# Attention and two expert layers on one core: four edits to the order of work around TensorE's waits

## Chip, cores and metric

The kernel runs on one core of a Trainium2 chip. The metric is the device time of one execution in microseconds (us), taken as the median of several. The engines are TensorE (PE in the profile, its weight loads PEld), VectorE (DVE), ScalarE (ACT), GpSimd (POOL) and SyncE (SP), which issues most transfers.

## What is computed

Three layers follow each other. The reference, cut to what matters:

```python
# 1. attention with a band mask: batch 4, 8 heads, 576 positions, head size 64
scores = (q @ k.T) / sqrt(64)          # heads 0-3: 32 back; heads 4-7: every fourth of 128 back
attn = softmax(where(mask, scores, -1e9))
x = (attn @ v) as [2304 tokens, 512]
# 2. a dense layer with squared ReLU: 512 -> 2048 -> 512
g = s * relu(x @ w_in) ** 2 + b
y = g @ w_out
# 3. eight experts, each token goes to one
logits = normalised(y) @ normalised(expert_emb).T / tau
e = argmax(logits);  gate = softmax(logits)[e]
out[token] = gate * (relu(y @ w1[e]) @ w2[e])
```

## The kernel before, in words

Every large product is made of three passes of TensorE: each operand is split into a rounded high part and a low part that holds the rest, and `mm3` (L459 to L463) adds high by high, and the two cross products. High parts are written by ScalarE, low parts by VectorE, so a product often waits for a low part.

**Groups, steps and slots.** The 2304 tokens are 18 tiles of 128 in five groups: g0 has 4 tiles, g1 has 2, g2 to g4 have 4 each. A group's dense layer has 16 steps, one for each 128 columns of the hidden size. A step has a first product (`gemm1_mm`, into a bank ph of PSUM, then ReLU, square and split) and, two steps later, a second product (`gemm2`), which adds into the group's banks py0 to py3, one for each tile; each py bank exists once. The steps run in the order g0's first half, all of g1, g0's second half, g2, g3, g4. The loop in `main` numbers half steps: slot 2i holds the first product of step i, slot 2i+1 the second product of step i-2. When a group's sixteenth second product is through, four copies (two for g1) take py to SBUF tiles ysb (L518). There are four ysb buffers in all, taken in turn, so a group's copies need the buffers that older groups' tiles leave.

**Attention beside it.** The attention of later groups is cut into pair units n = 8, 10, ... 34 and fitted into these slots by `attn_steps`. Each pair has a load (a), two sets of scores with their maximum and exponentials (b, scores pS by L241, maximum L248 and L251, exponentials L256), a normalisation (norm, L261 to L263), a turn of both probability tiles by transposes into banks pT with their copies (c, L270 and L274), the product with v and the high half of x (d, L284 and L301), and the low half of x (e, L305). `TEMPO` gives a start slot, a period and the offset of c for each group; steps of one slot come in the order a, d, e, c, b, norm. The probability tiles (tag prob) have two buffers; scores, turns and ph take four banks of PSUM in turn.

**Background items.** When a group's y has been copied, `logits_dve` puts a list of items on `self.bg`: for each tile eight dot products with the expert embeddings (VectorE, L761, one instruction of 512 columns each), then a choice of the expert (`choose`, L816 on) and gates. Behind the attention steps of a slot one item is taken from this list (two in odd slots from step 48 on, two in every slot in g4's steps). A group's ysb buffers are free when their last dot has run.

**What sets the order.** TensorE's instructions run in the order in which the program writes them. VectorE's and ScalarE's order in this part is chosen by the scheduler, with one exception: a dot is kept in program order, behind the VectorE instruction that the program wrote just before it. So a dot in a slot whose steps end with norm stands behind that normalisation.

**Experts.** From step 75 on, routing and the first expert's weights are prepared beside the last steps. Then TensorE turns gathered tokens (`xt`, banks px), makes hidden layers (`g1_pair` and `g1`, banks ph) and the second product (`g2`, banks po); `g2` scales po by the gate on VectorE (L1164) and scatters the rows to the output by an indirect transfer that GpSimd issues (L1165). At the very end a count of used slots is read into a register of each engine (`values_load`, L1312) and decides by a branch (L1314) whether more tokens are left; with this data none are.

Of the kernel before, what the change touches and what calls it, by code (L numbers as in the profile page):

```python
# [7 lines left out]
F32 = mybir.dt.float32  # L8
# [3 lines left out]
AF = mybir.ActivationFunctionType  # L12
# [8 lines left out]
NPOS = 2 * NPAIR + NSING + NTAIL  # L21
NUNIT = NPAIR + NSING + NTAIL
# [9 lines left out]
P = 128  # L32
# [77 lines left out]
class Kern:  # L110
# [277 lines left out]
    def attn_steps(self, n0, n1, ps):  # L388


        live = {}
        todo = []
        for n in range(n0, n1, 2):
            g = next(g for g in range(NG) if n // 4 < U0[g + 1])
            start, period, turn = TEMPO[g - 1]
            t = period * ((n - 4 * U0[g]) // 2) + start

            def a(n=n):
                ms = [divmod(n + i, 4) for i in range(2)]
                qks = [self.load_qk(*m) for m in ms]  # L400
                for i, m in enumerate(ms):
                    self.loaded[n + i] = qks[i], self.load_v(*m)
                live[n] = [self.attn_a(*m, ps) for m in ms]

            def each(*fs, n=n):
                def run(n=n):
                    for f in fs:
                        for c in live[n]:
                            f(c)
                return run  # L410

            def d(n=n):
                self.attn_pv(live[n])
                self.attn_hi(live[n])

            def e(n=n):
                self.attn_lo(live.pop(n))

            def b(n=n):
                self.attn_scores2(live[n])  # L420
                each(self.attn_max, self.attn_exp)(n)
            o = t + max(period, turn + 1)
            todo += [(t + LOAD, 0, n, a), (t, 4, n, b),
                     (t + 1, 5, n, each(self.attn_norm)), (t + turn, 3, n, each(self.attn_turn, self.attn_copy)),
                     (o, 1, n, d), (o + (turn < period), 2, n, e)]
        todo.sort(key=lambda x: x[:3])
        return todo
# [110 lines left out]

    def phase1(self, wl, first_pools, late, late_pools):
        tc, nc = self.tc, self.nc  # L540
        self.gt, self.bg, self.ysb, self.raws, self.loaded, self.py = {}, [], {}, {}, {}, {}
        sp_cm = tc.tile_pool(name="sp", bufs=1, side="right")
        self.spool = sp_cm.__enter__()
        ET = mybir.EngineType
        late.enter_context(tc.manual_schedule(engines={ET.PE}))
        with tc.tile_pool(name="psM", bufs=1, space=PSUM, reuse_waits="tile") as self.psM, ExitStack() as man:
            psA_cm = tc.tile_pool(name="psA", bufs=1, space=PSUM, side="right", reuse_waits="tile")
            self.psR = psA_cm.__enter__()
            self.turns, self.psf, self.step = [0, 1, 2, 3], self.bank_a, 0
            man.enter_context(tc.manual_schedule(engines={ET.Activation, ET.DVE}))  # L550
            with tc.tile_pool(name="pp", bufs=1) as self.ppool:
                self.warm = self.ppool.tile([P, 768], BF16, tag="prob", name="warm", bufs=5)[:, :P]
                nc.vector.memset(self.warm, 0.0)
                qk, v = {}, {}
                for n, what in FIRST:
                    if what == "w":
                        self.weight_load(n)
                    elif what == "s":
                        self.sb = self.lpool.tile([P, 2], F32, name="sb")
                        nc.sync.dma_start(out=self.sb[:, 0:1], in_=self.s.partition_broadcast(P))  # L560
                        nc.sync.dma_start(out=self.sb[:, 1:2], in_=self.b.partition_broadcast(P))
                    elif what == "q":
                        qk[n] = self.load_qk(*divmod(n, 4))
                    else:
                        v[n] = self.load_v(*divmod(n, 4))
                self.loaded = {n: (qk[n], v[n]) for n in qk}
                banks = [(self.psR, f"pa{i}") for i in range(4)] + [(self.psM, f"py{i}") for i in range(4)]

                def bank(name):
                    banks.append(banks.pop(0))  # L570
                    return banks[-1][0].tile([P, 512], F32, tag=banks[-1][1], name=name, bufs=1)
                conv = self.attn_first(bank)
                self.attn_consts(self.mask_pool, (0, 16, 32, 48, -16))
                man.close()
                conv.high()
                conv.low()
            self.x_half(wl)
            self.main(sp_cm, psA_cm, first_pools, late_pools)

    def main(self, sp_cm, psA_cm, first_pools, late_pools):  # L580
        tc, nc, wi = self.tc, self.nc, NPREP
        with tc.tile_pool(name="mp", bufs=2, reuse_waits="tile") as self.mpool:
            steps = self.attn_steps(8, 4 * NU, self.bank_a)
            slot, early = 0, []
            for i in range(NSTEP + LA):
# [33 lines left out]
                for kind in range(2):  # L619
                    if kind == 0 and i < NSTEP:  # L620
                        self.gemm1_mm(*ORDER[i], range(4) if i else (3,))
                        self.gemm1_act(*ORDER[i])
                        self.gemm1_low(*ORDER[i])
                    if kind == 1 and i >= LA:
                        self.gemm2(*ORDER[i - LA])
                    while steps and steps[0][0] < slot + 1:
                        steps.pop(0)[3]()
                    for _ in range(2 if i >= 16 * (NG - 1) else 1 + kind if i >= 48 else 1):
                        if self.bg:
                            self.bg.pop(0)()  # L630
                    slot += 1
                guard.close()
# [474 lines left out]
    def g1_pair(self, js, xh, xl, w):  # L1107

        nc = self.nc
        hh, hl = self.hidden(js)  # L1110

        def part(n, hook=None):
            ph = self.psE.tile([P, 2, 256], F32, tag="h", name=f"ph{js[0]}_{n}", bufs=3)
            for i in range(2):
                if i and hook:
                    hook(2 * n)
                fs = slice(P * (2 * n + i), P * (2 * n + i) + P)
                for k in range(4):
                    self.mm3(ph[:, i], w[0][k][:, fs], w[1][k][:, fs], xh[:, k], xl[:, k], k == 0, k == 3)
            ns = slice(2 * n, 2 * n + 2)  # L1120
            nc.scalar.activation(hh[:, ns], ph, AF.Relu)
            nc.vector.scalar_tensor_tensor(out=hl[:, ns], in0=ph, scalar=0.0, in1=hh[:, ns].bitcast(F32),
                                           op0=ALU.max, op1=ALU.subtract)
            if hook:
                hook(2 * n + 1)
        return (hh, hl), part
# [24 lines left out]
            nc.vector.tensor_sub(l, p3, h.bitcast(F32))  # L1151
        return hh, hl

    def g2(self, j, n, hh, hl, w, hook=None):
        nc = self.nc
        po = self.psE.tile([P, 512], F32, tag="o", name=f"po{j}", bufs=2)
        ts = slice(P * n, P * n + P)
        for k in range(8):
            fs = slice(512 * (k % 2), 512 * (k % 2) + 512)
            self.mm3(po, hh[:, k, ts], hl[:, k, ts], w[2][k // 2][:, fs], w[3][k // 2][:, fs], k == 0, k == 7)  # L1160
            if hook:
                hook(k)
        o = self.pad.tile([P, DM], F32, tag="o", name=f"o{j}", bufs=2)
        nc.vector.tensor_scalar_mul(o, po, self.gate[j])  # L1164
        nc.gpsimd.indirect_dma_start(out=self.out, out_offset=bass.IndirectOffsetOnAxis(ap=self.sidx[j], axis=0),  # L1165
                                     in_=o, in_offset=None, bounds_check=NT - 1, oob_is_err=False)

# [26 lines left out]
    def experts(self):  # L1194
# [91 lines left out]
        def hook(plan):  # L1286
            return lambda i: upto(*plan[i]) if i in plan else None

        with tc.manual_schedule(engines={mybir.EngineType.Activation, mybir.EngineType.DVE}):
            for u in range(1, nstat, 2):  # L1290
                more = u + 1 < nstat
# [5 lines left out]
                        gather(u + 2)  # L1297
                if more:
                    xt(u + 1)
                self.g2(runs[u][0], 0, *hts, w[u], hook({2: (u + 1, 5), 6: (u + 1, 6)}))  # L1300
                if more:
                    hs = self.g1(runs[u + 1][0], *xts.pop(u + 1), w[u + 1], hook({0: (u + 1, 7), 1: (u + 1, 8)}))
                self.g2(runs[u][1], 1, *hts, w[u], hook({2: (u + 2, 1), 6: (u + 2, 2)}))
                if more:
                    if u + 3 < nstat:
                        gather(u + 3)
# [2 lines left out]
                    self.g2(runs[u + 1][0], 0, *hts, w[u + 1],  # L1309
                            hook({1: (u + 2, 3), 3: (u + 2, 4), 5: (u + 2, 5), 7: (u + 2, 6)}))  # L1310
        assert not due
        used = nc.values_load(self.sexp[0:1, NUNIT:NUNIT + 1], min_val=0, max_val=2 * NPOS,  # L1312
                              skip_runtime_bounds_check_because="a count of slots, made by comparisons")
        with tc.If(used > 2 * NPAIR + NSING):  # L1314
            gather(nstat)
            for r in range(nstat, len(runs)):
# [62 lines left out]
```

## Time and profile before

| | |
|---|---|
| runs | 731.25, 732.04, 733.55 us; median 732.04 us |
| profiled execution, own time | 732.05 us |
| its span, first to last instruction | 730.3 us |
| mean granted clock of TensorE | 0.997 of full |

A row of the timeline gives the start in the span, the duration, the engine, the line, the operation, its output and inputs, the shape, the count of instructions merged into the row, and in brackets how long the engine stood still before it and what released it. Matmuls of one row overlap: two that follow each other at full speed start 0.23 us apart in the large products although each is shown with 0.39 us. So a wait of TensorE is read best as the distance of two starts, less 0.23. [...]

### The profile page before, as it was taken

The page shows a single profiled execution, that of the slowest core. Times are in us where ns is not written, and L with a number is a line of the kernel's source. Part 1 is how long each engine was busy: PE and PEld are TensorE (multiplying, and loading weights), DVE is VectorE, ACT ScalarE, POOL GpSimd, SP SyncE. Part 2 cuts the span into 40 slices and gives each one's busy share as a digit, 9 for nine tenths or more (in the row PEclk, how much of TensorE's full clock was granted, in tenths as well). Part 3 has the DMA queues.
Part 4 walks back from the last instruction along what each step waited for, and adds up shares of the span by engine and source line. Part 5 has one row for each costly group of instructions (what it writes and reads, how often), then busy time and mean ns, then how long its engine had stood idle before and what let it go on. Part 6 is the DMA issues. An engine that isn't in the chain of part 4 may idle for free. (4 is left out here: it accounts for less than half of the span.)

```text
span 730.3 us, 13189 instructions
## 1 busy us (share of the span) xinstructions
PE 716.1 (98%) x4763; PEld 603.5 (83%) x4763; DVE 530.1 (73%) x1228; ACT 388.7 (53%) x847; POOL 61.4 (8%) x94
## 2 busy tenths in 40 slices
PE   8999999999999999999999999999999999999996
PEld 6677898787888888888888888888888898989895
DVE  6999998775776645877836779369668686968671
ACT  6899886755644434444424226425246565656550
POOL 5000000000000000000000000204213131311011
PEclk9999999999999999999999999999999999999998
DMA  9765754421211101111001006304263077878610
GB/s 265 219 197 206 208 168 162 118 82 52 94 53 59 53 22 44 52 53 59 23 1 57 1 1 230 116 1 144 74 202 102 30 242 257 308 255 290 216 40 27
DMA packets 34039, 87.34 MB, mean 120 GB/s; under 512 B 4326, under 2 KB 4326, under 8 KB 33840
## 3 DMA queue, kind: packets, MB, share of 16 engines
q1 hardware_dynamic: 30608, 76.22, 32.3%
q0 software_dynamic: 3360, 10.23, 4.2%
q8 instruction: 39, 0.64, 0.4%
q14 instruction: 32, 0.26, 0.1%
HBM read 92.72 MB, written 10.22 MB: 141 GB/s over the span
## 5 line engine op out<-in xcount | busy, mean ns | idle before, releaser
L1075 DVE TENSOR_TENSOR wl<-raw,wh 128x1024 fp32r<-128x1024 f32 x96 | 113.8, 1221 | 29.3 <-ACT wh L1074 29.3
L461 PE MATMUL ph<-xhi,wih 128*128 128x512 f32 (+1 forms) x320 | 118.8, 371 | 0.0
L462 PE MATMUL ph<-xlo,wih 128*128 128x512 f32 (+1 forms) x320 | 117.7, 368 | 0.4 <-DVE xlo L305 0.4
L463 PE MATMUL ph<-xhi,wil 128*128 128x512 f32 (+1 forms) x320 | 117.7, 368 | 0.4 <-DVE wil L107 0.4
L461 PE MATMUL py<-woh,gh 128*128 128x512 f32 x288 | 115.2, 400 | 0.0
L462 PE MATMUL py<-wol,gh 128*128 128x512 f32 x288 | 112.7, 391 | 0.3 <-DVE wol L107 0.3
L463 PE MATMUL py<-woh,gl 128*128 128x512 f32 x288 | 112.3, 390 | 0.5 <-DVE gl L498 0.5
L1074 ACT CAST wh<-raw 128x1024 fp32r<-128x1024 f32 x96 | 96.2, 1055 | 8.7 <-DMA raw<-in_moe_w 8.7
L479 ACT ACTIVATE r<-ph 128x512 f32<-128x512 f32 (+1 forms) x80 | 44.2, 553 | 96.3 <-PE ph L463 95.9
L500 DVE SCALAR_TENSOR_TENSOR gl<-r,sb,gh 128x512 fp32r<-128x512 f32 (+1 forms) x56 | 39.9, 712 | 53.4 <-ACT gh L489 53.0
L761 DVE CUSTOM_DVE_ANT_0 junk<-ysb,enb 128x512 bf16<-128x512 f32 x112 | 77.0, 687 | 1.3
L489 ACT ACTIVATE gh<-r,sb 128x512 fp32r<-128x512 f32 (+1 forms) x56 | 38.8, 692 | 64.8 <-PE py L462 56.5
L461 PE MATMUL ph<-xh,wh 128*128 128x256 f32 x256 | 72.2, 282 | 0.7 <-ACT ysb L518 0.7
L462 PE MATMUL ph<-xl,wh 128*128 128x256 f32 x256 | 71.7, 280 | 0.0
L463 PE MATMUL ph<-xh,wl 128*128 128x256 f32 x256 | 71.7, 280 | 0.0
L461 PEld LDWEIGHTS ph<-xhi,wih 128*128 128x128 f32 x320 | 60.1, 188 | 11.2 <-ACT ysb L518 0.4
L463 PEld LDWEIGHTS ph<-xhi,wil 128*128 128x128 f32 x320 | 60.1, 188 | 11.0 <-DVE wil L107 1.0
L462 PEld LDWEIGHTS ph<-xlo,wih 128*128 128x128 f32 x320 | 60.1, 188 | 11.0 <-DVE xlo L305 0.9
L461 PE MATMUL po<-wh,hh 128*128 128x512 f32 x168 | 66.4, 396 | 0.0
L463 PE MATMUL po<-wh,hl 128*128 128x512 f32 x168 | 65.5, 390 | 0.0
L462 PE MATMUL po<-wl,hh 128*128 128x512 f32 x168 | 65.4, 389 | 0.0
L463 PEld LDWEIGHTS py<-woh,gl 128*128 128x128 f32 x288 | 54.1, 188 | 12.6 <-DVE gl L498 0.9
(304 smaller groups left out, 1261.5 us busy)
## 6 DMA issues: line engine op xcount, KB each, us to landing
raw<-in_moe_w SPq DMA_DIRECT2D x96, 512.0 KB
raw<-in_moe_w_in SPq DMA_DIRECT2D x16, 512.0 KB
raw<-in_moe_w_out SPq DMA_DIRECT2D x16, 512.0 KB
v<-in_vw SPq DMA_DIRECT2D x32, 192.0 KB
qk<-in_qkd SPq DMA_DIRECT2D x18, 320.0 KB
ydram<-ysb SPq DMA_DIRECT2D x18, 256.0 KB
qk<-in_qkp SPq DMA_DIRECT2D x15, 272.0 KB
enb<-in_moe_expert_emb SPq DMA_DIRECT2D x1, 2048.0 KB
```

Of the source, the lines that this page charges most:

```text
L461: nc.tensor.matmul(out, lhsT=ah, rhs=bh, start=first, stop=False)
L462: nc.tensor.matmul(out, lhsT=ah, rhs=bl, start=False, stop=False)
L463: nc.tensor.matmul(out, lhsT=al, rhs=bh, start=False, stop=last)
L479: nc.scalar.activation(r, ph, AF.Relu)
L489: nc.scalar.activation(gh, r, AF.Identity, bias=self.sb[:, 1:2])
L500: nc.vector.scalar_tensor_tensor(out=gl, in0=r, scalar=self.sb[:, 1:2], in1=gh.bitcast(F32), op0=ALU.add, op1=ALU.subtract)
L761: ins = nc.vector.tensor_tensor_reduce(out=self.junk, in0=y, in1=self.enb[:, e], scale=1.0, scalar=0.0, op0=ALU.mult, op1=ALU.add, accum_o ...
L1074: nc.scalar.copy(h, r)
L1075: nc.vector.tensor_sub(l, r, h.bitcast(F32))
```

## The change

There are four edits.

1. In `attn_steps` the whole pair n = 12 (the first of g2; 4*U0[2] is 12) starts one slot later: scores in slot 51, norm in 52, c in 54, d and e in 55. Its load moves from slot 45 to 46.
2. A flag `hold` is set when step c of a group's last pair has been written, and reset in its step e. While it is set no background item is taken. By the order of slots this skips one item in slot 62 (g2's last pair), three in slots 88 to 90 (g3's), and the items of slots 122 to 124 (g4's). All later items move back by that many.
3. In `g1_pair`, for the first pair of expert tiles, a tile of PSUM with the tag px is allocated and not used, ahead of the first ph.
4. In the last unit of experts `g2` scales the first 256 columns of po on VectorE and the other 256 on ScalarE; and the `values_load` of the count moves from behind the loop over the units to ahead of it.

```diff
@@ attn_steps
             t = period * ((n - 4 * U0[g]) // 2) + start
+            t += n == 4 * U0[2]
...
+            def c(n=n, g=g):
+                each(self.attn_turn, self.attn_copy)(n)
+                self.hold = n + 2 == 4 * U0[g + 1]
+
             def e(n=n):
                 self.attn_lo(live.pop(n))
+                self.hold = False
...
-                     (t + 1, 5, n, each(self.attn_norm)), (t + turn, 3, n, each(self.attn_turn, self.attn_copy)),
+                     (t + 1, 5, n, each(self.attn_norm)), (t + turn, 3, n, c),
@@ main
-                        if self.bg:
+                        if self.bg and not self.hold:
                             self.bg.pop(0)()
@@ g1_pair
+        if 0 in js:
+            self.psE.tile([P, 512], F32, tag="px", name="bank_px", bufs=1)
+
@@ g2
-    def g2(self, j, n, hh, hl, w, hook=None):
+    def g2(self, j, n, hh, hl, w, hook=None, two=False):
...
-        nc.vector.tensor_scalar_mul(o, po, self.gate[j])
+        c = DM // 2 if two else DM
+        nc.vector.tensor_scalar_mul(o[:, :c], po[:, :c], self.gate[j])
+        if two:
+            nc.scalar.activation(o[:, c:], po[:, c:], AF.Copy, scale=self.gate[j])
@@ the loop over expert units
+        used = nc.values_load(self.sexp[0:1, NUNIT:NUNIT + 1], min_val=0, max_val=2 * NPOS,
+                              skip_runtime_bounds_check_because="a count of slots, made by comparisons")
         with tc.manual_schedule(engines={mybir.EngineType.Activation, mybir.EngineType.DVE}):
...
-                self.g2(runs[u][0], 0, *hts, w[u], hook({2: (u + 1, 5), 6: (u + 1, 6)}))
+                self.g2(runs[u][0], 0, *hts, w[u], hook({2: (u + 1, 5), 6: (u + 1, 6)}), not more)
...
-                self.g2(runs[u][1], 1, *hts, w[u], hook({2: (u + 2, 1), 6: (u + 2, 2)}))
+                self.g2(runs[u][1], 1, *hts, w[u], hook({2: (u + 2, 1), 6: (u + 2, 2)}), not more)
...
-        used = nc.values_load(self.sexp[0:1, NUNIT:NUNIT + 1], min_val=0, max_val=2 * NPOS,
-                              skip_runtime_bounds_check_because="a count of slots, made by comparisons")
```

## Rows read from the trace of the kernel before

**Rows 1.** The page's busy times: each engine's us, share of span, instructions.

```profile
PE 716.1 (98%) x4763; PEld 603.5 (83%) x4763; DVE 530.1 (73%) x1228; ACT 388.7 (53%) x847; POOL 61.4 (8%) x94
```

**Rows 2.** Timeline at the first pair of g2: PE, then a later maximum on DVE.

```profile
128.48 0.38 PE L241 MATMUL pS<-qk 64*64 64x96 f32 x2
129.23 0.88 PE L241 MATMUL pS<-qk 64*64 64x96 f32 x30 [0.38 <-ACT r L479]
...
139.54 0.55 DVE L248 SCALAR_TENSOR_TENSOR prob<-pS,maskNone 128x384 f32<-128x384 f32 x1
```

**Rows 3.** Timeline at g2's last low half: PE, then DVE.

```profile
178.02 0.39 PE L461 MATMUL ph<-xhi,wih 128*128 128x512 f32 x1
...
178.84 0.50 PE L462 MATMUL ph<-xlo,wih 128*128 128x512 f32 x1 [0.44 <-DVE xlo L305]
...
177.50 0.68 DVE L761 CUSTOM_DVE_ANT_0 junk<-ysb,enb 128x512 bf16<-128x512 f32 x1
...
178.10 0.69 DVE L305 TENSOR_TENSOR xlo<-po,xhi 128x512 fp32r<-128x512 f32 x1
```

**Rows 4.** Timeline at the y copies of g0: DVE, ACT, PE.

```profile
193.72 0.56 DVE L263 TENSOR_TENSOR prob<-prob,st 128x384 f32<-128x384 f32 x1
...
193.17 0.57 ACT L518 COPY ysb<-py 128x512 f32<-128x512 f32 x1
...
194.12 0.39 PE L461 MATMUL py<-woh,gh 128*128 128x512 f32 x1
```

**Rows 5.** Timeline at the y copies of g2: DVE, ACT, PE.

```profile
290.21 0.69 DVE L761 CUSTOM_DVE_ANT_0 junk<-ysb,enb 128x512 bf16<-128x512 f32 x1
...
290.94 0.19 DVE L816 TENSOR_TENSOR rel<-dots,ef 128x32 f32<-128x32 f32 x1
...
298.05 0.55 DVE L263 TENSOR_TENSOR prob<-prob,st 128x384 f32<-128x384 f32 x1
298.52 0.68 DVE L761 CUSTOM_DVE_ANT_0 junk<-ysb,enb 128x512 bf16<-128x512 f32 x1
...
291.10 0.58 ACT L518 COPY ysb<-py 128x512 f32<-128x512 f32 x1
...
293.53 0.40 PE L461 MATMUL py<-woh,gh 128*128 128x512 f32 x1
```

**Rows 6.** Windows at the end; then 128x512 matmuls of line 310 (ns, min/median/max).

```profile
724.00:726.00 2.00, 0.00 (x0) 0.00 (x0) 0.45 (x1) 0.00 (x0) 0.85 (x1) 0.93 0.05 12
726.00:728.00 2.00, 0.00 (x0) 0.00 (x0) 0.00 (x0) 0.00 (x0) 0.14 (x1) 0.50 0.21 81
...
L310 PE MATMUL hot<-warm x5: 607/631/631, 1.1 to 2.8; 128*128 128x512 bf16 x5
L310 PE MATMUL pT<-identb x4: 379/379/389, 8.5 to 9.2; 128*128 128x512 bf16 x4
```

**Rows 7.** Timeline at the first expert product: PE, then ACT.

```profile
470.73 0.39 PE L463 MATMUL py<-woh,gl 128*128 128x512 f32 x1
471.80 0.39 PE L461 MATMUL ph<-xh,wh 128*128 128x256 f32 x1 [0.68 <-ACT ysb L518]
...
469.08 2.67 ACT L518 COPY ysb<-py 128x512 f32<-128x512 f32 x4
```

**Rows 8.** Timeline of the last two scatters and of a halved copy.

```profile
718.26 0.75 DVE L1164 TENSOR_SCALAR o<-po,gater 128x512 f32<-128x512 f32 x1 [4.12 <-PE po L463]
723.70 0.75 DVE L1164 TENSOR_SCALAR o<-po,gater 128x512 f32<-128x512 f32 x1 [4.69 <-PE po L463]
...
719.29 0.98 POOL L1165 DMA_INDIRECT out<-o,sidxr  x1 [14.23 <-DVE o L1164]
725.15 0.98 POOL L1165 DMA_INDIRECT out<-o,sidxr  x1 [4.88 <-DVEq L1314]
...
480.83 0.41 DVE L790 COPY dT<-pw 128x256 f32<-128x256 f32 x1
481.27 0.37 ACT L791 COPY dT<-pw 128x256 f32<-128x256 f32 x1 [1.09 <-DVE dT L790]
```

More of the change, by code (lines that the diff above doesn't have):

```diff
@@ L540, in phase1 @@
         tc, nc = self.tc, self.nc
+        self.hold = False
         self.gt, self.bg, self.ysb, self.raws, self.loaded, self.py = {}, [], {}, {}, {}, {}
```

## The prediction

> **What bounds the kernel now.** The page's busy times come first: TensorE is busy for 716.1 of 730.3 us [rows 1]. So nothing that another engine saves counts unless it ends a wait of TensorE, and each wait added to TensorE's fixed order is paid in full. The second view is the list of what TensorE waited for; it leads to four short waits, and the timeline at each shows what to see there. At g2's first scores two small matmuls start at 128.48 and the other 30 only 0.75 later; 30 of them take 0.88, so two should take 0.06, and the loss is 0.69 us; the release is the ReLU that reads the bank the scores want [rows 2]. At a first product the second pass starts 0.82 behind the first where 0.23 is normal, a loss of 0.59; VectorE runs a dot from 177.50 and only then, at 178.10, the low half that TensorE needs [rows 3]. At the first expert product the distance is 1.07, a loss of 0.84, and the release is a copy of y, the last of four in a row from 469.08: the product's bank is that of the tile copied last [rows 7]. At the end the last scatter starts 0.70 behind its scaling (723.70 and 0.75 make 724.45), the one before it 0.28 behind (719.01) [rows 8]: 0.42 more.
>
> **The change, part by part.**
>
> *One pair later.* The scores of n = 12 no longer stand behind that ReLU: -0.69. But only this pair moves, and the next keeps slot 53. Its scores now come ahead of the turn of n = 12 (slot 54), where before the turn came first in slot 53. There are two probability buffers, both still full with n = 12. So the next pair's maximum must wait for the transposes of the first tile, and with the four banks taken in turn (two scores, one ph, two turns) the second tile's turn takes the bank that this maximum reads. TensorE stands still between the two turns for one maximum of 0.55 [rows 2] and two hops between engines, each 0.05 by the step from the low half's end at 178.79 to the matmul at 178.84 [rows 3]: +0.65. Bounds: 0, if the buffers turn otherwise, and +1.34, if one more VectorE instruction of 0.69 [rows 3] is in front. The pair's load, issued a slot later on SyncE's queue, is hidden by the five slots between load and scores, which both move. Pair: **-0.04**.
>
> *The held items, gain.* The dot in front of g2's last low half goes; the half runs from 177.50, is done 0.60 earlier, and TensorE wants it 0.59 earlier [rows 3]: **-0.59** (0 if another VectorE instruction fills the gap). What is late next is the dot itself.
>
> *The held items, first price.* One item skipped in slot 62 moves g1's last dot from slot 66 to 67. There it stands behind the norm of pair 20, whose last multiply ends at 193.72 + 0.56 = 194.28 [rows 4]. The dot (0.68) ends at 194.96, and only then is its ysb buffer free for g0's fourth copy, of 0.57 as at 193.17: 195.53. g2's second product begins in slot 69 and needs that bank for its fourth tile at 194.12 [rows 4]: **+1.41**. Bounds: 0, if norm comes 1.4 earlier without the dots, and 2.1, with one more instruction of 0.7 ahead.
>
> *The held items, second price.* With the three of slots 88 to 90, four items are behind. g0's last two dots ran in slots 98 and 99, the last until 290.90; then came g2's fourth copy (it takes g0's last buffer) at 291.10, and g3's second product used that bank from 293.53 [rows 5]: 1.85 to spare. Now both dots fall into slot 101, behind the norm of pair 28. What a dot of that slot does is in the rows: the one that stood there before started at 298.52, at the norm's last multiply (298.05) and not sooner [rows 5]. Nothing cuts that short, since the copy waits for the dot, the dot for the norm, and TensorE, in order, for the copy. By these rows the two dots end at 298.60 + 2 x 0.68 = 299.96 and the copy at 300.54: a stall of 7.0. VectorE is rid of g0's choice and gates, though, of which 22 small instructions of 0.13 to 0.21 stood between 290.94 and that multiply; if ten of them, at 0.16, were in its way the stall is 5.4, and with another 0.7 ahead it is 7.7. I take **+6.4**, relief for four of them, as the multiply also waits for its exponentials. g4's skipped items cost nothing: g2's dots then end some slots before the next copies ask for their buffers.
>
> *The clock.* In all of before it is full but for the ends. [...] Coming back costs: at the start the 128x512 matmuls took 607 to 631 ns from 1.1, and 379 at 8.5 [rows 6]. How fast it came back between these is not in one row; between half speed for 0 and for the 7.4 us between these rows the loss is 0 to 3.7, half of the time. I take **+2.1**, a little over the middle, as work there was dense. [...]
>
> *The bank.* The unused tile takes the bank of the late copy, so the first product's is that of the first of four copies, done by 469.08 + 2.67 / 4 = 469.75, before 470.96 when it is wanted [rows 7]: **-0.84**. All that follows hangs on this product and moves along; it is 0 if the next copy or a transfer ends last.
>
> *The last gates.* The count's load leaves the end; if it made the 0.42, that is saved, and its own cost earlier is hidden by TensorE's work (0 if the wait was for the landing of the scatter before). The two halves don't run side by side: in the one place that already halves a bank's copy, ScalarE started at 481.27, when VectorE's half of 0.41 from 480.83 was done [rows 8]. So the halves take 0.81 from start to end against 0.75 whole: +0.06. [...] With halves side by side the part would be -0.76. I take **-0.36** (-0.42 to +0.06).
>
> **Sum:** -0.04 - 0.59 + 1.41 + 6.40 + 2.10 - 0.84 - 0.36 = +8.08 on the profiled execution's 732.05 gives **740.1 us**. That execution stands 0.01 above the median shown. A measurement of this kernel can tell 0.3%, 2.2 us, from no change.
>
> **Rivals.**
>
> *The stall comes, the clock holds.* Then 740.1 - 2.1 = 738.0. For it: the clock is full in all of before, through waits of under 1 us. Against: the fall at the end. Chance 0.28.
>
> *The dots aren't in the way*, the other sign. The place is g0's last dot in slot 101; if VectorE runs it by 292.9, so that the copy (0.58) is done by 293.5, there is no stall, and the same holds for g1's in slot 67. Then -0.04 - 0.59 - 0.84 - 0.36 = -1.83: 730.2; without the new wait between the turns, 729.6. For it: the copies are ordered by a scheduler, which might order the dots otherwise. Against: dots stay in program order, and the one at 298.52 sat exactly behind its multiply [rows 5]. Chance 0.14, of which 0.05 under 729.8.
>
> *Only the first price is paid*, where the second pair of dots slips in ahead of norm: 730.2 + 1.4 = 731.6. Chance 0.08.
>
> *The change does not do what it says*: the pair's wait is only moved. That is in the forecast already.
>
> **How the numbers follow.** The forecast, stall with a lower clock, has 0.50, and its own range is 737.5 to 743.5. The low end of the whole is the stall's lower bounds without the clock: -0.04 - 0.59 + 0 + 5.4 - 0.84 - 0.42 = +3.5, 735.6, and 735.0 without the wait between the turns. The high end adds to 740.1 what the stalls (0.7 and 1.3) and the clock (1.6) may take more, 743.7; not all come together: 743.5. Outside lie the two last rivals, 0.22. Faster 0.05 and same 0.09 from the third case, same 0.08 from the fourth, slower 0.78 from the first two.
>
> **What would show it.** Right: TensorE's list of waits has y's second product waiting for ysb's copy with about 6 us, near 293; a window there has a granted clock under 1; the dot that precedes the copy starts at the end of a multiply of L263; a smaller wait of the same kind near 194; in the pair's stretch no wait for the ReLU, but one of transposes; no wait at the first expert product; the last scatter about 0.3 behind its scaling. Wrong: no wait near 293, or dots of g0 ahead of the scores' maximum there.

## The result and the profile after

The changed kernel takes 740.41 us (median of 6, 739.87 to 742.08), the kernel before 731.67 in the same comparison: a ratio of 1.0116, with a 95% interval of 1.0099 to 1.0133. The forecast was 740.1. The profiled execution took 740.85 us with a span of 739.1, so it is 8.8 us longer than the one of before.

The list of what TensorE waited for, two of its rows, of the kernel after (columns: who waited, for whom, us in total, times, the longest):

```profile
PE py L467 <- ACT ysb L524: 7.3, 2, 6.0
...
PE pT L270 <- DVE prob L248: 0.7, 1, 0.7
```

The first row is new: twice, 7.3 us in all, the second product of the dense layer stood still for a copy of y. The row with L248 is new too. Three rows of before that the prediction named are gone: the scores' wait for the ReLU, the first product's for the low half and the first expert product's for a copy.

The large stall in the timeline of the kernel after: VectorE's dots and the norm, ScalarE's copy, TensorE.

```profile
297.61 0.17 DVE L261 TENSOR_SCALAR st<-st 128x4 f32<-128x4 f32 x1 [0.46 <-ACT prob L256]
...
298.02 0.56 DVE L263 TENSOR_TENSOR prob<-prob,st 128x384 f32<-128x384 f32 x1
298.50 0.69 DVE L768 CUSTOM_DVE_ANT_0 junk<-ysb,enb 128x512 bf16<-128x512 f32 x1
...
299.23 0.69 DVE L768 CUSTOM_DVE_ANT_0 junk<-ysb,enb 128x512 bf16<-128x512 f32 x1
...
299.96 0.59 ACT L524 COPY ysb<-py 128x512 f32<-128x512 f32 x1 [2.39 <-DVE dots L768]
...
294.17 0.39 PE L469 MATMUL py<-woh,gl 128*128 128x512 f32 x1
300.60 0.80 PE L467 MATMUL py<-woh,gh 128*128 128x512 f32 x1 [6.04 <-ACT ysb L524]
```

This answers to [rows 5], and the chain is read upwards: TensorE's matmul waits for the copy, the copy for the dot before it, both dots for the multiply of the norm, and the norm, in its first row, for ScalarE's exponentials. In [rows 5] the last dot was through at 290.90; here it starts at 299.23. The two starts of TensorE are 6.43 apart; less the usual 0.23 that is a loss of 6.2.

The windows around it, of the kernel after (columns, here and in [rows 6]: the stretch and its length in us; busy time and count of PE, PEld, DVE, ACT and POOL; granted clock of TensorE as a share of full; share of the transfer engines; GB/s):

```profile
296.00:298.00 2.00, 0.00 (x0) 0.00 (x0) 1.25 (x5) 1.57 (x10) 0.00 (x0) 0.87 0.00 0
298.00:300.00 2.00, 0.00 (x0) 0.00 (x0) 1.91 (x6) 0.04 (x1) 0.00 (x0) 0.50 0.00 0
300.00:302.00 2.00, 1.40 (x3) 1.16 (x4) 1.67 (x13) 1.53 (x5) 0.00 (x0) 0.50 0.31 120
302.00:304.00 2.00, 2.00 (x6) 1.56 (x5) 1.89 (x12) 0.58 (x1) 0.00 (x0) 0.50 0.03 11
304.00:306.00 2.00, 2.00 (x9) 1.59 (x9) 1.73 (x11) 0.00 (x0) 0.00 (x0) 0.93 0.01 4
306.00:308.00 2.00, 2.00 (x11) 1.64 (x10) 1.05 (x3) 0.60 (x1) 0.00 (x0) 1.00 0.00 0
```

The clock falls to 0.50 in the stall, at about 297.5, and stays there until about 304.3, for 3.7 us of work: the stretch from 302 has 6 large matmuls in 2 us, one at full clock has 11. That is how a stall charges a second time.

The smaller places, in the timeline of the kernel after: the turns of pair 12 and the maximum between them; the passes at g2's last low half and VectorE's row for it; the norm, the dot, g0's fourth copy and the two matmuls around its wait; the first expert product.

```profile
139.96 0.60 PE L270 MATMUL pT<-ident,prob 128*96 128x128 f32 x4
141.21 0.64 PE L270 MATMUL pT<-ident,prob 128*96 128x128 f32 x4 [0.65 <-DVE prob L248]
140.60 0.56 DVE L248 SCALAR_TENSOR_TENSOR prob<-pS,maskNone 128x384 f32<-128x384 f32 x1
...
177.84 0.39 PE L467 MATMUL ph<-xhi,wih 128*128 128x512 f32 x1
178.06 0.49 PE L468 MATMUL ph<-xlo,wih 128*128 128x512 f32 x1
177.31 0.68 DVE L305 TENSOR_TENSOR xlo<-po,xhi 128x512 fp32r<-128x512 f32 x1
...
192.97 0.56 DVE L263 TENSOR_TENSOR prob<-prob,st 128x384 f32<-128x384 f32 x1
193.45 0.69 DVE L768 CUSTOM_DVE_ANT_0 junk<-ysb,enb 128x512 bf16<-128x512 f32 x1
...
194.17 0.59 ACT L524 COPY ysb<-py 128x512 f32<-128x512 f32 x1
...
193.14 0.39 PE L469 MATMUL py<-woh,gl 128*128 128x512 f32 x1
194.81 0.50 PE L467 MATMUL py<-woh,gh 128*128 128x512 f32 x1 [1.28 <-ACT ysb L524]
...
479.65 0.39 PE L469 MATMUL py<-woh,gl 128*128 128x512 f32 x1
479.88 0.28 PE L467 MATMUL ph<-xh,wh 128*128 128x256 f32 x1
```

Four steps of the forecast can be checked here. Between the two turns VectorE's maximum runs from 140.60 to 141.16, and TensorE waits just for it (the wait of [rows 2] is gone, this one stands in its place). The low half is in time, if only just: it ends at 177.99, and the two passes start 0.22 apart, at 177.84 and 178.06, where [rows 3] had 0.82. The dot at 193.45, behind the norm's multiply from 192.97, brings the copy to 194.17; TensorE's starts are 1.67 apart, a stall of 1.4 [rows 4]. And the first expert product follows 0.23 behind the last second product, where [rows 7] had 1.07.

The end of the kernel after, timeline of the last scaling's halves and the scatter:

```profile
732.23 0.48 DVE L1175 TENSOR_SCALAR o<-po,gater 128x256 f32<-128x256 f32 x1 [4.96 <-PE po L469]
...
732.74 0.47 ACT L1177 ACTIVATE o<-po,gater 128x256 f32<-128x256 f32 x1 [4.96 <-DVE o L1175]
...
733.49 0.98 POOL L1178 DMA_INDIRECT out<-o,sidxr  x1 [4.46 <-DVEq L1327]
```

The halves run one behind the other, 0.98 in all against 0.75 for the whole, and the scatter starts 0.28 behind the second, where [rows 8] had 0.70.

### The profile page after: what moved, and what is told of

Its sections match the earlier page's. It is cut to its first block, busy times and chain, and to the rows that moved or that the text cites. A ratio compares the mean times of both kernels' runs of the same rounds, so it can differ in the third digit from the quotient of the medians.

```text
span 739.1 us, 13195 instructions
## 1 busy us (share of the span) xinstructions
PE 719.1 (97%) x4763; PEld 605.5 (82%) x4763; DVE 530.8 (72%) x1228; ACT 390.1 (53%) x849; POOL 61.5 (8%) x94
## 5 line engine op out<-in xcount | busy, mean ns | idle before, releaser
L467 PEld LDWEIGHTS py<-woh,gh 128*128 128x128 f32 x288 | 54.2, 188 | 19.5 <-ACT ysb L524 8.2
```

The source lines that it names most:

```text
L467: nc.tensor.matmul(out, lhsT=ah, rhs=bh, start=first, stop=False)
```

## The experiments

Times are medians; the kernel before stood at 732.30 (first four), 732.25 (next four) and 732.05 us (last three) in the same comparisons. Its executions lie between 731.15 and 733.73, so steps of half a microsecond are read from the profiles, and the medians only say whether the whole fits. In the profile of the kernel before TensorE waited 0.9 for a first transfer at 7.7, and most of the other profiles are 0.3 to 0.9 ahead of it from there on; so profiles are compared place by place and not by their totals.

### Without the flag

```diff
...
-                        if self.bg and not self.hold:
+                        if self.bg:
```

> All of the change but the flag: no background item is skipped. Theory: the two stalls (1.45 and 6.2 us) and the low clock behind the second come from the skipped items alone, so the time falls from 740.4 to the kernel before with the pair (-0.1), the bank (-0.8, and +0.4 of slower products behind it) and the end (+0.3): 731.0 to 731.8, and TensorE waits at no copy of y. Rival: the pair or the bank moves the buffers of PSUM so that the copies come late; then most of the 8.7 us stays, above 736.

Measured 732.01 us, a ratio of 0.9995 (0.9986 to 1.0004). The waits for a copy of y are gone from the list of TensorE's waits; what the flag was to remove is back, and the turn's wait for the maximum stays. Two rows of that list, of this kernel:

```profile
PE pT L270 <- DVE prob L248: 0.7, 1, 0.7
...
PE ph L466 <- DVE xlo L305: 0.4, 1, 0.4
```

So the flag alone makes the loss. The median is 0.2 above the range that was expected; its profiled execution, 730.87, is 0.1 below it.

### One item held, in slot 62

This and the next two edit the kernel before; only the slots differ.

```diff
-                        if self.bg:
+                        if self.bg and slot not in (62,):
```

> The kernel before with one item skipped, in slot 62. Theory: the low half comes 0.6 earlier and g1's last dot goes behind the norm of pair 20, which stalls TensorE for 1.4 near 194; g0's last dots move by one item only, into slot 99, ahead of the scores of pair 28, and cost nothing near 293. In sum +0.8 us, 732.3 to 732.8. Rival: every skipped item delays the copies of g2 by the same share, 6.2/4 = 1.6 us, so that it is near 734.2; or no dot is in the way of a copy: -0.6, 731.1.

Measured 732.33, a ratio of 1.0000 (0.9992 to 1.0009). In its list of TensorE's waits one second product waits for a copy of y, as none did in the kernel before, and the wait for the low half is gone:

```profile
PE py L461 <- ACT ysb L518: 1.3, 1, 1.3
```

The wait is the one near 194 (1.4 between starts); near 293 there is none. Both terms are there as forecast, -0.6 and +1.4; the median lies in the range expected, but beside the kernel before of the same runs their sum of 0.8 lies just above the interval's end (0.7), so the medians don't show the size of the sum. The profile does: beside the profile of the kernel before, TensorE's matmuls are 0.4 early ahead of the two places and 0.6 late behind them, 1.0 in all. The rival by the item, +1.9, is far outside; the rival without a wait falls with the row.

### Two items held, in slots 88 and 89

```diff
+                        if self.bg and slot not in (88, 89):
```

> The kernel before with two items skipped, in slots 88 and 89. Theory: what counts is the VectorE instruction that a dot stands behind. By two items g0's last dot goes into slot 100, behind the last reduction of pair 28 (done at 294.35 in the kernel before), so it ends near 295.0 and the copy near 295.6: a stall of 2.1 us and no fall of the clock, or a short one: 733.8 (to 735). Rival: lateness counts by the item: 3.1 us and a fall of the clock, 735.5; or nothing below three items.

Measured 737.41, a ratio of 1.0068 (1.0054 to 1.0083): the theory's 733.8 and the rival's 735.5 were both too low. The wait for the copy is 3.7 between starts instead of 2.1. The timeline of this kernel, VectorE's last dot of g0, then ScalarE:

```profile
293.61 0.68 DVE L761 CUSTOM_DVE_ANT_0 junk<-ysb,enb 128x512 bf16<-128x512 f32 x1
...
295.78 0.36 ACT L256 ACTIVATE prob<-prob,st 128x96 f32<-128x96 f32 x1
296.14 0.56 ACT L518 COPY ysb<-py 128x512 f32<-128x512 f32 x1
```

The dot stands where it was expected, behind the reduction, and is done at 294.3. But the copy starts only at 296.14: ScalarE has the eight exponentials of the same pair ahead of it, from 293.26 on. So a second queue has a part in it, which the expectation had left out: here the copy starts when its dot is done and ScalarE's exponentials are through. With three or four items late the dot ends after the exponentials, and the queue doesn't show. In the profiled execution the clock falls too, although the stall is shorter: the windows of this kernel have 0.79 and then 0.50 up to 302, and TensorE loses a further 2.6 there.

```profile
294.00:296.00 2.00, 0.00 (x0) 0.00 (x0) 1.84 (x12) 2.00 (x12) 0.00 (x0) 0.79 0.06 22
296.00:298.00 2.00, 1.25 (x3) 1.06 (x4) 1.78 (x13) 1.46 (x6) 0.00 (x0) 0.50 0.22 87
...
300.00:302.00 2.00, 2.00 (x6) 1.55 (x5) 1.03 (x7) 0.00 (x0) 0.00 (x0) 0.50 0.01 4
```

The other three executions have a mean granted clock of 0.996, 0.997 and 0.997, against 0.993 in the profiled one and 0.992 to 0.994 in all six of the changed kernel. So by the record the clock fell for less time in them, or not at all, although they took about as long (737.12 to 737.82). The stall explains 3.7 of the 5.1 us in the median; what makes up the rest in those executions stays open.

### Three items held, in slots 88 to 90

```diff
+                        if self.bg and slot not in (88, 89, 90):
```

> The kernel before with three items skipped, in slots 88 to 90. Theory: g0's last dot alone goes into slot 101, behind the last multiply of pair 28's norm, so the stall is that of the change less one dot, 6.2 - 0.7 = 5.5 us, with a clock of 0.5 behind it for 1.8 us: 739.0 (738.3 to 739.7). Rival: lateness counts by the item: 4.7 us, 738.1 or less; no wait near 194 and the low half late at 178 as before in either.

Measured 739.64, a ratio of 1.0093 (1.0078 to 1.0109). The wait is 5.5 between starts, as the theory had it: one dot less than in the changed kernel. By the item it would have been 4.7. The list of waits of this kernel:

```profile
PE py L461 <- ACT ysb L518: 5.3, 1, 5.3
```

One, two, three and four items late give stalls near 293 of 0, 3.7, 5.5 and 6.2: no straight line, but steps, each set by the instruction behind which the last dot stands, or by the queue of the copy.

### TensorE kept at work in the stall

```diff
+            if (g, fc, i) == (3, 0, 2):
+                for _ in range(24):
+                    self.nc.tensor.matmul(self.py[g][i], lhsT=gh[:, ts], rhs=self.woh[fc], start=True, stop=True)
             self.mm3(self.py[g][i], gh[:, ts], gl[:, ts], self.woh[fc], self.wol[fc], fc == 0, fc == 15)
```

> The changed kernel with 24 extra matmuls of 128x512 ahead of the third tile of g3's first second product, into that tile's bank, whose first real matmul then clears it. They keep TensorE at work for 24 x 0.23 = 5.5 us of the 6.2 in which it stood still for g2's fourth copy of y. Theory: the granted clock stays full and the 1.8 us of slow matmuls behind the stall go, while the wait itself is as long as before: 740.4 - 1.8 = 738.6 (738.2 to 739.0), with a wait of some 0.7 left. Rival: the matmuls behind the stall are slow for another reason (transfers, banks) and the time stays at 740.4; or the extra matmuls delay the copy and it is longer.

Measured 738.66, a ratio of 1.0091 (1.0075 to 1.0106), 1.75 us below the changed kernel. The windows of this kernel keep the full clock through the place:

```profile
298.00:300.00 2.00, 1.72 (x8) 1.10 (x6) 1.90 (x7) 0.32 (x1) 0.00 (x0) 1.00 0.00 0
300.00:302.00 2.00, 1.68 (x7) 1.42 (x8) 1.63 (x11) 1.84 (x5) 0.00 (x0) 1.00 0.34 131
302.00:304.00 2.00, 2.00 (x10) 1.65 (x10) 2.00 (x15) 0.00 (x0) 0.00 (x0) 1.00 0.00 0
```

The copy came as late as before (TensorE went on at 300.32, the changed kernel at 300.60), so the stall's own price stayed, and only the slow stretch behind it went. By the two profiles that is worth 1.7 us. The medians differ by 1.75, but the kernel before of this comparison stood 0.6 higher, so beside it the gain is 2.3. Two of the five executions, the profiled one and the longest, have a lower mean clock (0.995, the others 0.997): in the profile it fell at another place, which the last section shows.

### The load of the count alone

```diff
+        used = nc.values_load(self.sexp[0:1, NUNIT:NUNIT + 1], ...)
         with tc.manual_schedule(engines={mybir.EngineType.Activation, mybir.EngineType.DVE}):
...
-        used = nc.values_load(self.sexp[0:1, NUNIT:NUNIT + 1], ...)
```

> The kernel before with the load of the count ahead of the loop over units, nothing else. Theory: the last scatter waits for GpSimd's queue, which is held until the scatter before has landed (4.5 to 5.0 us) and 0.53 longer; with the load moved off TensorE's queue that landing takes 3.1 us, as in the run without the flag, and the last scatter starts 0.28 behind its scaling instead of up to 0.70: 0 to 0.5 us faster, 731.6 to 732.1 beside 732.0. Rival: the halves did it, and here the scatter before still lands after 4.5 us or more.

Measured 731.81, a ratio of 0.9997 (0.9986 to 1.0008): nothing that the medians can tell. In the profile the last scatter starts 0.27 behind its scaling (723.39 + 0.75 to 724.41):

```profile
723.39 0.75 DVE L1164 TENSOR_SCALAR o<-po,gater 128x512 f32<-128x512 f32 x1 [4.69 <-PE po L463]
...
724.41 0.98 POOL L1165 DMA_INDIRECT out<-o,sidxr  x1 [4.46 <-DVE o L1164]
```

GpSimd's queue was held for the scatter before it for 3.4 us here. In the profiles with the load ahead of the loop it was 3.1 to 3.9 (3.2 in the changed kernel), in those with the load behind it 4.2 to 5.0 (5.0 in the kernel before); where the landing came last, the queue went on 0.53 behind it. That gates the last scatter in some executions (0.70 in [rows 8]), but not in all: in the run with slot 62 held the landing came 0.5 ahead of the scaling's end, and the distance was 0.28 with the load unmoved.

### The halves alone

```diff
...
+        c = DM // 2 if two else DM
+        nc.vector.tensor_scalar_mul(o[:, :c], po[:, :c], self.gate[j])
+        if two:
+            nc.scalar.activation(o[:, c:], po[:, c:], AF.Copy, scale=self.gate[j])
...
```

> The kernel before with the last unit's scaling in halves on VectorE and ScalarE, the load left where it was. Theory: ScalarE's half starts when VectorE's is done, so scaling takes 0.48 + 0.03 + 0.47 = 0.99 instead of 0.75, and the scatter before still lands after 4.5 to 5.0 us, which hides part of it: 0 to +0.25 us, 732.0 to 732.3. Rival: the halves shorten the landing of the scatter before, and it is 0.2 faster.

Measured 733.25, a ratio of 1.0008 (0.9998 to 1.0019). The profile has the halves in series and the scatter 0.27 behind them, as in the changed kernel:

```profile
722.83 0.48 DVE L1165 TENSOR_SCALAR o<-po,gater 128x256 f32<-128x256 f32 x1 [4.96 <-PE po L463]
...
723.35 0.47 ACT L1167 ACTIVATE o<-po,gater 128x256 f32<-128x256 f32 x1 [4.96 <-DVE o L1165]
...
724.09 0.98 POOL L1168 DMA_INDIRECT out<-o,sidxr  x1 [4.45 <-DVEq L1317]
```

So the halves cost 0.24 where they are (0.99 from start to end, 0.75 before), and if anything the kernel is slower by it. The median's 1.0 us is more than that, and its interval takes in no change; why it is so high stays open.

### The bank, and the hold made up for at once

```diff
-... else 1 + kind if i >= 48 else 1):
+... else 1 + kind if i >= 48 else {62: 0, 63: 2}.get(slot, 1)):
...
+        if 0 in js:
+            self.psE.tile([P, 512], F32, tag="px", name="bank_px", bufs=1)
```

> The kernel before with the unused bank ahead of the first expert product, no item in slot 62 and two in slot 63, so that nothing is late from slot 64 on. Theory: the wait of 0.6 at g2's last low half and that of 0.84 at the expert product go and no stall comes: -1.4 us, 730.6 (730.2 to 731.0). Rival: two dots in slot 63 delay VectorE where it now matters (a low part of g0's last steps) and give the 0.6 back: 731.2; or the wait at the expert product returns at the next product, 731.4.

Measured 731.46, a ratio of 0.9988 (0.9979 to 0.9998): faster, by less in the median (0.8) than the theory had (1.4). In the profile both waits are gone and no new one is there: the passes at the low half start at 177.64 and 177.87, and the first expert product 0.23 behind the last second product:

```profile
469.74 0.39 PE L463 MATMUL py<-woh,gl 128*128 128x512 f32 x1
469.97 0.28 PE L461 MATMUL ph<-xh,wh 128*128 128x256 f32 x1
```

### The whole change, with every hold made up for

```diff
...
-                        if self.bg and not self.hold:
+                        if self.bg and self.hold:
+                            owed += 1
+                        elif self.bg:
                             self.bg.pop(0)()
+                    if owed and self.bg and not self.hold:
+                        owed -= 1
+                        self.bg.pop(0)()
```

> The whole change with the flag kept, but each slot after a hold takes one item more until none is late (slot 63 for the one item, slots 91 to 93 for the three). Theory: it is the lateness in slots 67 and 101 that costs, not the holding, so the two stalls and the low clock go and the low half stays early: 740.4 - 1.45 - 6.2 - 1.8 = 730.9 (730.3 to 731.5), with no wait for a copy of y. Rival: two items in a slot delay other work of VectorE, and part of the gain of 0.6 at 178 is given back, or a new wait shows: above 731.7.

Measured 730.46, a ratio of 0.9978 (0.9970 to 0.9987): ten microseconds below the changed kernel, and below the kernel before. The list of TensorE's waits has no copy of y, no low half and no ReLU in it; only the turn's wait and the one at the second slot table are left of those that this text names:

```profile
PE ptabr L900 <- DVE btr L895: 0.7, 1, 0.7
PE pT L270 <- DVE prob L248: 0.7, 1, 0.7
```

This separates the two readings of the flag: holding an item does no harm here, leaving it late does.

### The gains put together

The edits of the run with the bank and slot 63, and the moved load.

> The kernel before with the unused bank, the hold in slot 62 made up for in slot 63, and the load of the count moved: the parts that each gained alone. Theory: -0.6 - 0.8 - 0.4 = -1.8 us beside the kernel before of the same runs, a ratio of 0.9975. Rival: the moved load gains nothing in the median, -1.0 to -1.4, 0.998 to 0.9988.

Measured 730.69, a ratio of 0.9986 (0.9974 to 0.9998). The fastest executions are at 730.0, those of the kernel before at 731.2, but some of this kernel are at 731.5 to 734.4, which the next run is about. The theory's 0.9975 is just inside the interval, and so is the rival.

### Matmuls at the second slot table

These come on top of the edits of the run before.

```diff
+        if nm == "r":
+            for _ in range(4):
+                nc.tensor.matmul(pt[:, :512], lhsT=self.w[0][0][0][:, :P], rhs=self.w[0][0][0][:, :512], start=True, stop=True)
```

> As catch_bank_load, with four matmuls of 128x512 ahead of the small ones of the second slot table, where TensorE stands still for 0.87 us and then makes 18 small matmuls. In the profiled execution of the run with the extra matmuls the granted clock fell to 0.5 some 2 us behind that place (24 matmuls at 0.213 us apart instead of 0.113 to 0.118, 2.4 us lost), and executions of the kernel before fall into two sets some 1.7 us apart. Theory: the short idle time lets the clock fall in some executions; the four matmuls (0.9 us, in 0.87 of idle time) prevent it: the slower set goes, the median falls by 0.5 to 1 us below catch_bank_load and the runs lie closer together. Rival: the two sets come from elsewhere (transfers at the start): the same median, or 0.1 to 0.3 more, and the same spread.

Measured 730.50, a ratio of 0.9976 (0.9968 to 0.9985). The wait for btr is no longer in the way; in the timeline of this kernel the four lie in front of the 18 small ones:

```profile
497.23 1.07 PE L888 MATMUL ptabr<-wh 128*128 128x512 f32 x4
498.14 1.63 PE L891 MATMUL ptabr<-btr,atr 128*128 128x48 bf16 x18
```

The median fell by only 0.2, less than the theory's 0.5 to 1; the spread is smaller as it had it, 729.77 to 731.65 against 729.99 to 734.39. That the clock falls at this place in some executions is shown in one profile (below); that this is what sets all the longer executions apart is not. The mean granted clock of each execution, which is on record, fits a fall somewhere: of the 81 executions of the kernel before, none of the 49 under 732.6 us has less than 0.997, and 18 of the 32 above have 0.994 to 0.996; of the run before three of twelve have less than 0.997, of this one none. It doesn't say where the clock fell.

## Why the prediction was right, step by step

The differences below are those of the two profiled executions, taken by how far each of TensorE's matmuls is behind its counterpart.

- **The pair.** -0.04 forecast, -0.06 measured over the stretch. The wait for the ReLU became a wait for the next pair's maximum, 0.8 between starts where 0.65 was worked out; that the sum came out so close is in part luck.
- **The low half.** -0.59 forecast, -0.59 measured.
- **The first stall.** +1.41 forecast, +1.44 measured between the two starts, behind the multiply that the forecast named. The passes right behind it start a little further apart, which makes it 1.6.
- **The second stall.** +6.4 forecast, +6.2 measured. The relief by VectorE's small instructions was a choice between bounds, and 0.6 was taken. TensorE reached the place 0.87 later than in the kernel before, and the multiply ran at 298.02 against 298.05 [rows 5], so the relief was 0.9. The rival that dots aren't in the way falls with the row at 298.50, at the norm's last multiply, and with the runs with two, three and no items held. g4's held items cost nothing, as forecast: from 300 to 460 the distance to the kernel before stays at 8.9.
- **The clock.** +2.1 forecast, +1.8 measured in the profile and +1.7 by the run that keeps TensorE at work. The 2.1 was a choice in a range of 0 to 3.7, so its closeness is luck. That the clock falls in a stall of 6 us was the author's estimate: the profile of before shows a fall only at its end, where TensorE's last matmul starts at 723.27 and the clock is 1.00 until 725.5 and then falls [rows 6]. The two runs show it at this place, with 0.50 in the idle stall (298 to 300) and 1.00 in the same stretch with work in it. The rival that the clock holds falls with the same windows.
- **The bank.** -0.84 forecast, -0.8 measured; no other copy or transfer took its place.
- **The last gates.** This is the term that was wrong: -0.36 forecast, +0.27 measured. The halves cost 0.24 and not 0.06, since a half with the gate takes 0.48 and 0.47 where the plain copies of [rows 8] took 0.41 and 0.37. The distance of 0.42 was won, but it was not a fixed cost: it depends on when the scatter before lands. And the last transfer itself held the queue 0.46 longer than in the profile of before; over the profiles that stretch took 2.6 to 3.1 us, whatever the edit, so this part is no work of the change. As forecast, the halves come in series: ScalarE's starts at 732.74, VectorE's lasts until 732.71, and in the run with the halves alone the two are at 723.35 and 723.31.
- **Not in the sum:** +0.4 at the products of the second pair of expert tiles, told in the last section.

The sum of 8.08 thus came out near the 8.8 of the two profiled executions with errors of 0.6, 0.4 and 0.2 on the same side and of 0.3 and 0.2 on the other. That 740.1 lies still closer to the median of 740.41 is luck: it was added to 732.05, and the kernel before stood at 731.67 in the comparison.

## What to carry to other kernels

An item of filler work has a due time: the buffer that it reads last is somebody's next output. Before moving such items back, follow the last of them to the buffer it frees and to the engine that runs in a fixed order and wants it, and count the place by the instruction behind which it will stand, not by the number of items. Where a hold is worth it, take the held items up again at once: here that turned 8.7 us lost into 1.6 won. And a stall of several microseconds of TensorE can be charged twice, the second time by the clock: 6.2 and 1.8 us here.

## What was unexpected

**The clock fell once without a long stall.** In the profiled execution of the run with 24 extra matmuls, TensorE stood still for 0.87 us (1.10 between starts, less 0.23) at the second slot table and then made 18 small matmuls; two windows on, the clock was at half. Sixteen matmuls there start 0.213 apart, and 1.7 us are lost; the expectation of the last run, with 24 and 2.4, counted too many. The windows of that kernel:

```profile
504.00:506.00 2.00, 1.37 (x7) 0.79 (x5) 2.00 (x10) 0.00 (x0) 0.00 (x0) 1.00 0.85 266
506.00:508.00 2.00, 1.92 (x21) 1.44 (x22) 2.00 (x11) 1.05 (x1) 0.00 (x0) 1.00 0.64 258
508.00:510.00 2.00, 2.00 (x14) 2.00 (x13) 1.93 (x7) 1.98 (x3) 1.26 (x2) 0.65 0.00 0
510.00:512.00 2.00, 2.00 (x11) 2.00 (x11) 2.00 (x4) 1.92 (x3) 1.69 (x2) 0.50 0.48 164
```

The kernel before has the same wait of 0.87 at that place and kept 1.00 there in its profile.

**The same products at two paces.** The 128x256 products of the second pair of expert tiles started 0.113 us apart in the profiles of the kernel before, of the run without the flag and of those with one or two items held, and 0.118 apart in those of the changed kernel and of the run with three held: 0.4 us over 96 of them. It goes neither with the unused bank nor with the number of bytes moved; what it goes with stays open.

**A shorter stall cost more clock, where the clock fell.** In the profiles the stalls of 3.7, 5.5 and 6.2 were followed by a further loss of 2.6, 2.1 and 1.8: eleven, eight and seven matmuls start about 0.43 apart there instead of 0.23. By the windows the clock was at 0.50 for about 6.8 us each time, and of these 1.6, 2.6 and 3.1 passed in the stall: the longer TensorE stood still, the more of the slow time passed there. But it didn't fall alike in every execution: in three of four with two items held, and in one of four with three held, the mean granted clock is 0.996 or 0.997.
